# Random-feature attention and two MLPs on one core: projections by head in half the array's rows, products in half its columns, squares of the first batch as products

## The chip, the cores and the metric

The kernel runs on one core of one Trainium2 chip. The time is the device time of one launch in microseconds, the median of several runs; lower is better. One further run is profiled.

## What is computed

Attention with positive random features (4 batches, 8 heads, 576 tokens, head size 64, 128 features) is followed by two MLPs without biases, 512 to 2048 to 512, on the 2304 tokens.

```python
q_s, k_s = (q * scale, k * scale)            # scale = 64 ** -0.25
def phi(x):
    proj = np.einsum('bhsd,md->bhsm', x, omega)
    sq = np.sum(x * x, axis=-1, keepdims=True) / 2.0
    h = proj - sq
    h = h - np.max(h, axis=-1, keepdims=True)
    return np.exp(h) / np.sqrt(m)
q_p, k_p = (phi(q_s), phi(k_s))
kv = np.einsum('bhsm,bhsd->bhmd', k_p, v)
z = np.sum(k_p, axis=2)
num = np.einsum('bhsm,bhmd->bhsd', q_p, kv)
den = np.einsum('bhsm,bhm->bhs', q_p, z)[..., None] + 1e-06
x = num / den                                # tokens x 512
x = softplus(x @ w_in) @ w_out               # first MLP
x = silu(x @ w_in2) @ w_out2                 # second MLP
```

## The kernel before, in words

**Blocks.** The first MLP goes over five token blocks: block b (0 to 3) has the 512 first tokens of batch b, block 4 the 4 x 64 tokens that are left. A block has 16 steps: `gemm1` makes 128 rows of the hidden layer (12 matmuls, three for each of four chunks, since a number is split into a high and a low float32r part), ScalarE applies the softplus twice (once rounded), VectorE takes the difference as the low part, and `gemm2` adds the step's part to four banks of PSUM (12 matmuls). The second MLP does the same with the SiLU on what the first one stored in DRAM.

**Attention.** What block b needs of the attention is computed while block b - 1 runs; that of block 0 before any MLP step, in what is called the opening here. It comes in halves: one half is 256 tokens by four heads of k or of q (`k_half`, `q_half`), or 128 tail tokens of two batches by eight heads (`k_tail`). For each half `inputs` loads x with the head dimension on the partitions (`xT`: two heads below each other, 64 rows each) and once more with tokens on the partitions (`xN`); ScalarE squares `xN` and VectorE sums the squares of each head (`sums`). `features` then works in two groups e:

- `project` (TensorE): features of two heads at once, `xT` as the 128 x 128 stationary operand and the block-diagonal 128 x 256 matrix `om_sb` as the moving one. [...] 
- `top` and `shift` (VectorE): the maximum of each token and head, and the bias from the maximum and the sum of squares in two small operations (L417, L418).
- the exponential (ScalarE): with the bias for each of four heads in batches 0 and 1 (L429), else after a VectorE addition, both groups in one instruction (L439, L446).

A half of k is multiplied with v and a column of ones (`kv`, L489; 65 columns move) and added to the sums `kvs` of its batch. A half of q is transposed (`flip`, L541, tiles `pq`), copied by ScalarE to `qt`, multiplied with `kvs` (`num`, L553, tiles `pn`), divided by its last column on VectorE (`norm`), transposed back (`back`, L575, tiles `px`) and split into the block's x. The tail of q does `num` in column halves (L557: 64 of 128 stationary columns each, for two batches).

**Order.** A class `Order` decides the order of the instructions of PE, ACT, DVE and SP ahead of time. Each item has an engine, a cost, what it depends on, tiles of rings (`BUFS`) and a due time that is propagated backwards; the item that can start first is taken, among equals that with the earliest due time. Weights are loaded as int64 words of float64 numbers and converted on ScalarE and VectorE (L284 to L301 and `diff`, L209), those of the first MLP mostly during block 0.

Of the kernel before, what the change touches and what calls it, by code (L numbers as in the profile page):

```python
# [18 lines left out]
P = 128  # L19
# [17 lines left out]
BUFS = {"wt": 16, "xt": 2, "ghl": 3, "b4": 4, "g": 2, "f": 2, "ld": 3, "b2": 4, "sq": 9, "mn": 6, "den": 3, "bank": 4, "y": 4}  # L37
# [3 lines left out]
G1, G2, G3 = 0.2267, 0.117, 0.224  # L41
# [4 lines left out]
PIPE = 0.25  # L46
RATE = 380e3
ARRIVE = 2.0
ISSUE = 0.5
BEGIN = 45.0  # L50


class Order:
# [5 lines left out]
    def add(self, eng, cost, fn, deps=(), due=None, alloc=(), uses=(), table=None, nbytes=0, after=0.0, loose=False, behind=None):  # L59
        occ, lag = cost if isinstance(cost, tuple) else (cost, PIPE)  # L60
        i = len(self.items)
        it = dict(
            i=i, eng=eng, occ=occ, lag=lag, fn=fn, deps=[d for d in deps if d is not None], due=due,
            alloc=list(alloc), table=table, nbytes=nbytes, after=after, loose=loose, behind=behind, start=None, end=None,
        )
# [9 lines left out]
    def propagate(self):  # L75
# [115 lines left out]
def attention_moe_moe_kernel(  # L191
# [18 lines left out]

    E = mybir.EngineType
# [8 lines left out]
    home = {"wt": pool, "xt": pool, "b4": pool, "ghl": pool, "g": odd, "f": odd, "ld": odd, "b2": odd, "sq": odd, "mn": odd, "den": odd, "bank": psum, "y": psum}  # L220
# [27 lines left out]
    for layer in range(2):  # L248
        for sb in range(NSB):
            full = width[sb] == 2 * T  # L250
            for fc in range(NFC):
                due1[layer, sb, fc] = t
                t += (24 * G1 if full else 12 * (G2 + (G1 / 2 if layer else G2))) + ((1.9 if sb else 2.2) if layer == 0 and sb < B else 0)
    due1["end"] = t

    def bits_pair():
        nc.scalar.copy(bd[:, 0], om_sb)
        diff(bd[:, 1], om_sb, bd[:, 0].bitcast(F32))
# [62 lines left out]
    def inputs(s, name, xT, xN, vs, simple, held, after):  # L321
# [25 lines left out]
        ln = add("SP", (ISSUE, 0), load_n, rv, alloc=[] if here else [tn], uses=[tn] if here else [], nbytes=P * 2048, after=after)  # L347
# [12 lines left out]
        def square():  # L360
            nc.scalar.activation(s["nat"], s["nat"], AF.Square)
# [4 lines left out]

        tsq = new("sq")
        sq = add("ACT", A5, square, [ln], uses=[tn])
        red = add("DVE", V5, sums, [sq], alloc=[tsq], uses=[tn])
        if simple:  # L370
            return lx, tx, red, tsq, lv, tv
        th = new("b4")

        def high():
            s["hl"] = get("b4", [P, 2, 512], F32R, f"hl_{name}")
            nc.scalar.copy(s["hl"][:, 0, :], s["xt"])

        def low():
            diff(s["hl"][:, 1, :], s["xt"], s["hl"][:, 0, :].bitcast(F32))

        h = add("ACT", A5, high, [lx], alloc=[th], uses=[tx])
        l = add("DVE", V5, low, [h], alloc=[], uses=[tx, th])
        return l, th, red, tsq, lv, tv

    def features(s, name, simple, ins, cols, sq_of, psums):
# [5 lines left out]
        for e in range(2):  # L391
            tp, tm = new(psums()), new("mn")

            def project(e=e, tp=tp):
                pp = s["pp", e] = get(tp["tag"], [P, 4, M], F32, f"pp_{name}_{e}")
                for i in range(2):
                    o = pp[:, 2 * i : 2 * i + 2, :].rearrange("p j m -> p (j m)")
                    cs = slice(cols[e][i], cols[e][i] + P)
                    if simple:
# [7 lines left out]
            def top(e=e):  # L407
                s["mn", e] = get("mn", [P, 8], F32, f"mn_{name}_{e}")
                nc.vector.tensor_reduce(s["mn", e][:, :4], s["pp", e], op=ALU.max, axis=AX.X)  # L409

            def shift(e=e):
                s["nb", e] = s["mn", e][:, 4:]
                m3 = s["mn", e][:, :4].rearrange("p (c j) -> p c j", c=2)
                n3 = s["nb", e][:, :4].rearrange("p (c j) -> p c j", c=2)
                sq = sq_of(s["sq"], e)
# [4 lines left out]
            p = add("PE", 4 * G3 if simple else 6 * G2, project, [x, const_ready], alloc=[tp], uses=[tx])  # L420
            m = add("DVE", V5, top, [p], alloc=[tm], uses=[tp])
            n = add("DVE", VS, shift, [m, red], uses=[tm, tsq])
            if simple:
                tphi = new("b2")

                def exp(e=e):
                    phi = get("b2", [P, 4, M], F32, f"phi_{name}_{e}")
                    for i in range(4):
                        nc.scalar.activation(phi[:, i], s["pp", e][:, i], AF.Exp, bias=s["nb", e][:, i : i + 1])  # L429
                    s["phi", e] = phi  # L430
# [4 lines left out]
            def shifted(e=e):  # L435
                if e == 0:
                    s["both"] = get("b4", [P, 2, 4, M], F32, f"phi_{name}")
                nb = s["nb", e][:, :4].unsqueeze(2).to_broadcast([P, 4, M])
                nc.vector.tensor_tensor(s["both"][:, e], s["pp", e], nb, op=ALU.add)  # L439

            adds.append(add("DVE", V5, shifted, [n] + adds, alloc=[tboth] if e == 0 else [], uses=[tp, tm] + ([tboth] if e else [])))
# [29 lines left out]
    def k_half(n, half, simple, psums, due, after):  # L471
# [3 lines left out]
        ins = inputs(s, name, kT[n, :, 2 * half : 2 * half + 2, :], kN[n, :, :, hs, :], [(v1[n, :, :, hs, :], (2, 4))], simple, simple, after)  # L475
        cols, sq_of = main_cols()
        phis = features(s, name, simple, ins, cols, sq_of, psums)
        tk = new(psums())
        b, h0 = n // 2, 4 * half
        both = []  # L480
        for e, (x, tphi) in enumerate(phis):

            def kv(e=e):
                phi, v = s["phi", e], s["v", 0]
                if "pkv" not in s:
                    s["pkv"] = get(tk["tag"], [P, 4, D + 1], F32, f"pkv_{name}")
                for j in range(2):
# [5 lines left out]
            both.append(add("PE", 4 * G3, kv, [x, ins[4][0]] + both, alloc=[] if e else [tk], uses=[tphi, ins[5][0]] + ([tk] if e else [])))  # L493
        chain(b, h0, add("DVE", VH, lambda: kv_add(b, h0, s["pkv"]), both, due=due, uses=[tk]))

    def k_tail(bp, simple, psums, due, after):
# [3 lines left out]
        ins = inputs(s, name, kT[NT, :, :, bp * P : (bp + 1) * P], kN[NT, :, bp], vs, simple, simple, after)  # L500
        cols = [(2 * u * P, 2 * u * P + P) for u in range(2)]
        phis = features(s, name, simple, ins, cols, lambda sq, u: sq[:, 4 * u : 4 * u + 4].rearrange("p (c j) -> p c j", c=2), psums)
        for u, (x, tphi) in enumerate(phis):
            for i in range(2):
                tk = new(psums())

                def kv(u=u, i=i, tk=tk):
                    phi, v = s["phi", u], s["v", u]
                    pkv = s["pkv", u, i] = get(tk["tag"], [P, 2, 2, D + 1], F32, f"pkv_{name}_{u}_{i}")
                    for j in range(2):  # L510
                        nc.tensor.matmul(
                            pkv[:, j].rearrange("p a d -> p (a d)"), phi[:, 2 * i + j, :],
# [3 lines left out]
                k = add("PE", 2 * G3, kv, [x, ins[4][u]], alloc=[tk], uses=[tphi, ins[5][u]])  # L516
# [5 lines left out]
    def q_half(n, half, simple, psums, due, after):  # L522
# [327 lines left out]
```

## Time and profile before

| | us |
|---|---|
| median of 3 runs | 972.95 (972.69 to 976.61) |
| profiled execution | 972.0 |
| its span, first to last instruction | 970.2 |
| TensorE busy | 943.5 (97%) |
| ScalarE busy | 443.3 (46%) |
| VectorE busy | 427.6 (44%) |
| mean granted TensorE clock | 0.994 of full speed |

Busy time counts the union of an engine's instructions. Matmuls overlap in their pipeline, so the duration of one is longer than its share of the stream; the distance between the starts of two is that share.

### The profile page before, as it was taken

What the parts mean: (1) busy time and instruction counts of PE and PEld (TensorE: products, weight loads), DVE (VectorE), ACT (ScalarE), POOL (GpSimd) and SP (SyncE); (2) the same over time, 40 slices, a digit from 0 to 9 for tenths busy, and PEclk for the clock granted to TensorE, in tenths of its full rate; (3) what the DMA queues carried; (4) which work ended last, traced back from release to release, by engine and by line L of the source; (5) the groups of instructions that cost most, each with busy time, mean ns of one, the idle gap of its engine ahead of it and who ended that gap; (6) DMA issues with size and microseconds to landing.
All of it is one profiled execution on the core that took longest, in us unless ns stands there. A gap on an engine that the chain in (4) does not pass through costs nothing.

```text
span 970.2 us, 12523 instructions
## 1 busy us (share of the span) xinstructions
PE 943.5 (97%) x4936; PEld 803.3 (83%) x4936; DVE 427.6 (44%) x923; ACT 443.3 (46%) x810; POOL 1.2 (0%) x7
## 2 busy tenths in 40 slices
PE   8899999999999999999999999999999999999994
PEld 7678778888888888887889988888888888888893
DVE  6987889455535453442112999521111112111210
ACT  7888878555555555442213776332222122221220
POOL 0000000000000000000000000000000000000000
PEclk9999999999999999999999999999999999999998
DMA  9643443222012221010003666202002000100100
GB/s 332 217 141 131 154 151 109 87 88 77 22 34 77 78 65 33 1 45 1 0 1 131 217 197 217 75 12 76 0 9 79 1 1 11 60 1 6 44 1 22
DMA packets 38159, 72.86 MB, mean 75 GB/s; under 512 B 3412, under 2 KB 18388, under 8 KB 38100
## 3 DMA queue, kind: packets, MB, share of 16 engines
q1 hardware_dynamic: 37970, 71.79, 22.0%
q8 instruction: 39, 0.64, 0.3%
q10 hardware_dynamic: 130, 0.26, 0.1%
q14 instruction: 20, 0.16, 0.1%
HBM read 62.60 MB, written 9.44 MB: 74 GB/s over the span
## 4 chain that ended last, share of the span: by engine, by line
PE 86%; DVE 5%; ACT 5%; DMA 2%; issue 1%; SPq 0%; ACTq 0%; DVEq 0%
PE y L664 20%; PE y L656 18%; PE h L633 13%; PE h L635 13%; PE h L634 13%; PE pkv_k L489 2%; PE pn_q L553 2%; PE pq_q L541 1%; DMA xN_q<-in_qN 1%; ACT phi_k L429 1%; DVE wt L209 1%; DVE wf L292 1%; ACT L641 1%; ACT L429 1%; PE px_q L575 1%
## 5 line engine op out<-in xcount | busy, mean ns | idle before, releaser
L209 DVE TENSOR_TENSOR ghl<-g,ghl 128x512 fp32r<-128x512 f32 (+1 forms) x160 | 101.9, 637 | 413.1 <-ACT ghl L642 411.6
L641 ACT ACTIVATE g<-h 128x512 f32<-128x512 f32 (+1 forms) x160 | 88.6, 554 | 333.4 <-PE h L635 332.9
L633 PE MATMUL h<-x,wt 128*128 128x512 f32 (+1 forms) x640 | 238.2, 372 | 0.4 <-ACT ghl L642 0.4
L634 PE MATMUL h<-x,wt 128*128 128x512 f32 (+1 forms) x640 | 235.8, 368 | 0.9 <-DVE x L209 0.9
L635 PE MATMUL h<-x,wt 128*128 128x512 f32 (+1 forms) x640 | 236.0, 369 | 0.0
L656 PE MATMUL y<-ghl,wt 128*128 128x512 f32 (+1 forms) x960 | 213.8, 372 | 0.0
L664 PE MATMUL y<-wt,ghl 128*128 128x512 f32 x864 | 208.6, 390 | 0.0
L656 PEld LDWEIGHTS y<-ghl,wt 128*128 128x128 f32 x960 | 166.2, 189 | 28.4
L664 PEld LDWEIGHTS y<-wt,ghl 128*128 128x128 f32 x864 | 161.3, 188 | 32.8
L634 PEld LDWEIGHTS h<-x,wt 128*128 128x128 f32 x640 | 120.8, 189 | 21.0 <-DVE x L209 1.3
L633 PEld LDWEIGHTS h<-x,wt 128*128 128x128 f32 x640 | 120.7, 189 | 20.4 <-ACT ghl L642 0.8
L635 PEld LDWEIGHTS h<-x,wt 128*128 128x128 f32 x640 | 120.7, 189 | 20.4
L642 ACT ACTIVATE ghl<-h 128x512 fp32r<-128x512 f32 (+1 forms) x160 | 88.1, 550 | 35.7 <-PE y L664 29.3
L284 ACT ACTIVATE wf<-raw 128x512 f32<-128x512 f32 x64 | 43.1, 681 | 13.8 <-DVE wt L209 13.5
L301 ACT CAST wt<-wf 128x512 fp32r<-128x512 f32 x64 | 39.4, 624 | 16.4 <-DVE wf L296 15.9
L209 DVE TENSOR_TENSOR wt<-wf,wt 128x512 fp32r<-128x512 f32 x64 | 43.2, 685 | 5.3 <-ACT wt L301 5.2
L292 DVE SCALAR_TENSOR_TENSOR wf<-wf,raw 128x512 uint32<-128x512 uint32 x64 | 43.0, 685 | 1.5 <-ACT wf L284 1.1
L296 DVE SCALAR_TENSOR_TENSOR wf<-raw,wf 128x512 uint32<-128x512 uint32 x64 | 43.1, 684 | 0.2
L641 ACT ACT_TABLE_LOAD x29 | 37.2, 1283 | 11.8 <-PE h L635 11.5
L409 DVE TENSOR_REDUCE mn_q<-pp_q 128x4 f32<-128x512 f32 x36 | 24.4, 686 | 24.3 <-PE pp_q L405 24.3
L553 PEld LDWEIGHTS pn_q<-kv,qt_q 128*128 128x128 f32 x256 | 30.8, 192 | 5.0 <-ACT qt_q L545 4.1
L553 PE MATMUL pn_q<-kv,qt_q 128*128 128x65 f32 x256 | 31.2, 275 | 2.4 <-ACT qt_q L545 2.4
(103 smaller groups left out, 708.8 us busy)
## 6 DMA issues: line engine op xcount, KB each, us to landing
raw<-in_w SPq DMA_DIRECT2D x64, 512.0 KB, 3.7
out<-y_sb SPq DMA_DIRECT2D x17, 256.0 KB, 2.2
y_dram<-y_sb SPq DMA_DIRECT2D x16, 256.0 KB, 2.0
x2raw<-y_dram SPq DMA_DIRECT2D x16, 256.0 KB, 3.8
xT_q<-in_qT SPq DMA_DIRECT2D x14, 256.0 KB, 2.9
xN_q<-in_qN SPq DMA_DIRECT2D x14, 256.0 KB, 3.1
x_k<-in_v SPq DMA_DIRECT2D x8, 260.0 KB, 5.3
v_k<-in_v SPq DMA_DIRECT2D x8, 260.0 KB, 3.0
```

The costliest lines, as they stand in the source:

```text
L209: nc.vector.tensor_tensor(o, a, b, op=ALU.subtract)
L284: nc.scalar.activation(s["f"], hif, AF.Copy, scale=2.0**-112)
L292: nc.vector.scalar_tensor_tensor(fu, fu, 3, lo, op0=ALU.logical_shift_left, op1=ALU.bitwise_or)
L296: nc.vector.scalar_tensor_tensor(fu, hi, 0x80000000, fu, op0=ALU.bitwise_and, op1=ALU.bitwise_or)
L553: nc.tensor.matmul(pn[:, i, :], qt[:, i, :], kvs[n // 2][:, h, :], start=True, stop=True)
L633: nc.tensor.matmul(ph[:, :w], wt[:, 0, 0, cs], xt[:, 0, cc, :w], start=(cc == 0), stop=False)
L634: nc.tensor.matmul(ph[:, :w], wt[:, 0, 0, cs], xt[:, 1, cc, :w], start=False, stop=False)
L635: nc.tensor.matmul(ph[:, :w], wt[:, 0, 1, cs], xt[:, 0, cc, :w], start=False, stop=(cc == NCC - 1))
L641: nc.scalar.activation(g, s["h"][:, :w], f)
L642: nc.scalar.activation(ghl[:, 0, :w], s["h"][:, :w], f)
L656: nc.tensor.matmul(py[dm][:, :w], wt[:, 1, a, cs], g[:, x, :w], start=(first and i == 0), stop=(last and i == 2),)
L664: nc.tensor.matmul(py[c], g[:, x, cs], wt[:, 1, a, :], start=(first and i == 0), stop=(last and i == 2),)
```

## The change

Eight edits:

1. `project` multiplies each head by itself: the 64 rows of `xT` that hold head j of a pair, with the same 64 rows of a 128-column omega (`om_sb` holds it twice, one below the other). The two heads of a pair follow each other, write different banks of PSUM and stand in different rows of the array. It is float32 in all batches; the split of x and omega (`hl`, `bd`) is gone. A half's groups are now its heads by parity j, four heads each.
2. In the first batch (`fold`: k and q of n < 2, and the first k tail) ScalarE squares `xT`, and a second product of the squares with a matrix of -scale^2/2 (`neg_half`) is added to the projection, so that the maximum alone, negated, is the bias. The load of `xN`, `sums` and `shift` are gone there.
3. `kv` of the main tokens and `num` of the main tokens are done in column halves by `by_halves`.
4. `project` is one item for both groups; it writes two banks. The flips wait for both groups' exponentials.
5. The features of batches 0 and 1 have a ring `ph` of their own (4); `ghl` has 2 buffers for 3, `b4` 3 for 4.
6. Projections of batch 0 use the ring `y` alone, everything else `bank`.
7. Planning: costs `G4`, extra lead `wait` (`AHEAD`, `WAIT`), `BEGIN` 36 for 45, 1.4 for 1.9 a step in blocks 1 to 3.
8. The second MLP's weights may be loaded from the start (`after` 0.0).

```diff
-BUFS = {"wt": 16, "xt": 2, "ghl": 3, "b4": 4, "g": 2, "f": 2, "ld": 3, "b2": 4, "sq": 9, "mn": 6, "den": 3, "bank": 4, "y": 4}
+BUFS = {"wt": 16, "xt": 2, "ghl": 2, "b4": 3, "g": 2, "f": 2, "ld": 3, "b2": 4, "ph": 4, "sq": 9, "mn": 6, "den": 3, "bank": 4, "y": 4}
...
+    def by_halves(o, a, b, **flags):
+
+        for c in range(2):
+            r = slice(c * 64, c * 64 + 64)
+            nc.tensor.matmul(o[r], a[:, r], b, **flags)
...
-    bd = const.tile([P, 2, 2 * M], F32R, name="bd")
-    om_sb = const.tile([P, 2 * M], F32, name="om_sb")
-    nc.sync.dma_start(om_sb, om)
+    om_sb = const.tile([P, M], F32, name="om_sb")
+    for j in range(2):
+        nc.sync.dma_start(om_sb[j * D : (j + 1) * D, :], om[j * D : (j + 1) * D, j * M : (j + 1) * M])
...
-        ln = add("SP", (ISSUE, 0), load_n, rv, alloc=[] if here else [tn], uses=[tn] if here else [], nbytes=P * 2048, after=after)
+        ln = None if fold else add("SP", (ISSUE, 0), load_n, rv, alloc=[] if here else [tn], uses=[tn] if here else [], nbytes=P * 2048, after=after)
...
-            nc.scalar.activation(s["nat"], s["nat"], AF.Square)
+            nc.scalar.activation(s["nat"], s["xt"] if fold else s["nat"], AF.Square)
...
-                    if simple:
-                        nc.tensor.matmul(o, s["xt"][:, cs], om_sb, start=True, stop=True)
-                    else:
-                        hl = s["hl"]
-                        nc.tensor.matmul(o, hl[:, 0, cs], bd[:, 0, :], start=True, stop=False)
-                        nc.tensor.matmul(o, hl[:, 0, cs], bd[:, 1, :], start=False, stop=False)
-                        nc.tensor.matmul(o, hl[:, 1, cs], bd[:, 0, :], start=False, stop=True)
...
+            for q, c in enumerate(cols):
+                for j in range(2):
+                    r = slice(j * D, (j + 1) * D)
+                    nc.tensor.matmul(pp[j][:, q], s["xt"][r, c : c + P], om_sb[r, :], start=True, stop=not fold)
+                if fold:
+                    for j in range(2):
+                        r = slice(j * D, (j + 1) * D)
+                        nc.tensor.matmul(pp[j][:, q], s["nat"][r, c : c + P], neg_half[r, :], start=False, stop=True)
...
+                if fold:
+                    s["nb", j] = s["mn", j]
+                    nc.vector.tensor_reduce(s["mn", j][:, :4], s["pp"][j], op=ALU.max, axis=AX.X, negate=True)
...
-                        nc.tensor.matmul(
-                            s["pkv"][:, 2 * e + j], phi[:, 2 * c + j, :], v[:, c, 2 * e + j, :], start=(c == 0), stop=(c == 1)
-                        )
+                        by_halves(s["pkv"][:, 2 * e + j], phi[:, 2 * e + c, :], v[:, c, 2 * e + j, :], start=(c == 0), stop=(c == 1))
...
-                        nc.tensor.matmul(pn[:, i, :], qt[:, i, :], kvs[n // 2][:, h, :], start=True, stop=True)
+                        by_halves(pn[:, i, :], qt[:, i, :], kvs[n // 2][:, h, :], start=True, stop=True)
...
-                    weights(1, fc, io, due1[0, NSB - 1, 0] + 2.8 * fc + 2.0)
+                    weights(1, fc, io, 0.0)
```

What this does to the order is seen in three places. The first is the start of VectorE's list; `mn` are the maxima, `sqs` the sums of squares, `pp` the projections. Before:

```order
L409 TENSOR_REDUCE mn_k_0_0_123<-pp_k_0_0_114 128x4
L365 TENSOR_REDUCE sqs_k_0_126<-x_k_0_94 128x8
L409 TENSOR_REDUCE mn_k_0_1_133<-pp_k_0_1_120 128x4
L417 SCALAR_TENSOR_TENSOR mn_k_0_0_123<-sqs_k_0_126,mn_k_0_0_123 128x4
L418 SCALAR_TENSOR_TENSOR mn_k_0_0_123<-sqs_k_0_126,mn_k_0_0_123 128x4
L417 SCALAR_TENSOR_TENSOR mn_k_0_1_133<-sqs_k_0_126,mn_k_0_1_133 128x4
L418 SCALAR_TENSOR_TENSOR mn_k_0_1_133<-sqs_k_0_126,mn_k_0_1_133 128x4
```

And now, the first two halves:

```order
L414 TENSOR_REDUCE mn_k_0_0_159<-pp_k_0_0_117 128x4
L414 TENSOR_REDUCE mn_k_0_1_165<-pp_k_0_1_118 128x4
L414 TENSOR_REDUCE mn_k_0_0_179<-pp_k_0_0_140 128x4
L414 TENSOR_REDUCE mn_k_0_1_192<-pp_k_0_1_141 128x4
L469 COPY kv_90<-pkv_k_0_181 128x260
```

Of seven operations for a half of the first batch two are left.

The second is on TensorE in block 0, around its ninth step; `y` is gemm2 (four rows are one), `pn` the product of q features with the sums, `px` the transposition back. Before:

```order
L656 MATMUL y_0_3_797<-ghl_0_7_1240,wt_7_1059 128x512 x3
L553 MATMUL pn_q_1_0_1357<-kv_89,qt_q_1_0_1333 128x65 x4
L553 MATMUL pn_q_1_1_1364<-kv_89,qt_q_1_1_1348 128x65 x4
L633 MATMUL h_0_9_1377<-x_0_487,wt_9_1229 128x512
L634 MATMUL h_0_9_1377<-x_0_487,wt_9_1229 128x512
L635 MATMUL h_0_9_1377<-x_0_487,wt_9_1229 128x512
```

Nine more rows of that gemm1 (`h_0_9`) stand ahead of the `px` that reads what VectorE made of `pn`. Now:

```order
L659 MATMUL y_0_3_915<-ghl_0_7_1386,wt_7_1313 128x512 x3
L217 MATMUL pn_q_1_0_1503<-kv_91,qt_q_1_0_1474 64x65 x8
L217 MATMUL pn_q_1_1_1521<-kv_91,qt_q_1_1_1489 64x65 x8
L578 MATMUL px_q_1_1532<-ident,xn_q_1_0_1517 128x128 x2
L397 MATMUL pp_q_0_0_1536<-om_sb,xT_q_0_1199 128x128
L397 MATMUL pp_q_0_1_1537<-om_sb,xT_q_0_1199 128x128
L397 MATMUL pp_q_0_0_1536<-om_sb,xT_q_0_1199 128x128
L397 MATMUL pp_q_0_1_1537<-om_sb,xT_q_0_1199 128x128
```

The `px` follows the second `pn` at once, and the gemm1 of that step comes after the next gemm2.

The third is on TensorE one step later: the flips `pq` of the last half of q in block 0, whose projection `pp_q_1` is the first row. Now:

```order
L397 MATMUL pp_q_1_1_1696<-om_sb,xT_q_1_1419 128x128
L578 MATMUL px_q_0_1690<-ident,xn_q_0_1_1688 128x128 x2
L659 MATMUL y_0_0_912<-ghl_0_9_1623,wt_9_1519 128x512 x3
L659 MATMUL y_0_1_913<-ghl_0_9_1623,wt_9_1519 128x512 x3
L659 MATMUL y_0_2_914<-ghl_0_9_1623,wt_9_1519 128x512 x3
L659 MATMUL y_0_3_915<-ghl_0_9_1623,wt_9_1519 128x512 x3
L544 MATMUL pq_q_1_0_1757<-ident,phi_q_1_0_1737 128x128
```

Before, a whole gemm1 (twelve rows) stood between that gemm2 and the flips; now it comes after them.

## Rows read from the trace of the kernel before

**Rows 1.** Busy time by stage (columns in the first row): opening, blocks 0 to 4.

```profile
core 0: us, PE busy (x) PEld busy (x) DVE busy (x) ACT busy (x) POOL busy (x), PEclk, DMA share, GB/s
0.00:53.94 53.94, 47.10 (x276) 38.77 (x277) 44.11 (x127) 40.31 (x109) 1.16 (x7) 0.97 0.76 262
53.94:177.23 123.29, 119.85 (x619) 100.77 (x618) 100.08 (x222) 99.91 (x189) 0.00 (x0) 1.00 0.38 128
177.23:301.65 124.42, 124.42 (x697) 108.15 (x696) 61.75 (x149) 66.70 (x92) 0.00 (x0) 1.00 0.19 60
301.65:417.54 115.89, 115.89 (x645) 100.36 (x644) 56.85 (x132) 62.74 (x87) 0.00 (x0) 1.00 0.17 53
417.54:513.79 96.25, 93.98 (x485) 77.75 (x484) 19.75 (x40) 27.30 (x45) 0.00 (x0) 1.00 0.03 11
513.79:559.72 45.93, 45.93 (x373) 45.44 (x372) 30.27 (x60) 25.51 (x57) 0.00 (x0) 1.00 0.53 184
```

**Rows 2.** The same columns for the opening from its sixth microsecond on.

```profile
20.00:34.00 14.00, 13.20 (x89) 11.50 (x87) 13.35 (x47) 12.29 (x37) 0.00 (x0) 1.00 0.97 348
34.00:53.94 19.94, 16.60 (x102) 13.76 (x103) 18.63 (x51) 14.72 (x36) 0.00 (x0) 0.91 0.45 147
sum 47.94, PE 42.87 PEld 36.67 DVE 43.69 ACT 37.80 POOL 0.00; mean PE 14.29 PEld 12.22 DVE 14.56 ACT 12.60 POOL 0.00
```

**Rows 3.** Timeline of TensorE in the opening: start, duration, instructions merged.

```profile
15.88 1.08 PE L400 MATMUL pp_k<-om_sb,x_k 128*128 128x256 f32 x4
16.80 1.00 PE L489 MATMUL pkv_k<-x_k,phi_k 128*128 128x65 f32 x8
17.64 1.08 PE L400 MATMUL pp_k<-om_sb,x_k 128*128 128x256 f32 x4
```

**Rows 4.** Timeline in block 1: split projections.

```profile
203.83 0.29 PE L405 MATMUL pp_k<-bd,hl_k 128*128 128x256 f32 x1
...
204.19 0.28 PE L405 MATMUL pp_k<-bd,hl_k 128*128 128x256 f32 x1
```

**Rows 5.** Chain that ended last, in order of time: start, duration.

```profile
484.03 2.72 PE y L656 x12
```

**Rows 6.** Timeline in block 3 around the column halves (PEld: weight loads).

```profile
447.54 0.39 PE L635 MATMUL h<-x,wt 128*128 128x512 f32 x1
447.85 1.01 PEld L557 LDWEIGHTS pn_q<-kv,qt_q 128*64 128x64 f32 x32 [0.35 <-issue]
...
449.14 0.69 DVE L209 TENSOR_TENSOR ghl<-g,ghl 128x512 fp32r<-128x512 f32 x1 [4.25 <-ACT ghl L642]
...
450.72 0.30 PE L575 MATMUL px_q<-ident,xn_q 128*128 128x128 f32 x1 [1.71 <-DVE den_q L564]
```

**Rows 7.** Durations of line L557: ns min/median/max.

```profile
L557 PEld LDWEIGHTS pn_q<-kv,qt_q x64: 132/138/142, 424.0 to 448.7; 128*64 128x64 f32 x64
```

**Rows 8.** Timeline of VectorE in the opening.

```profile
7.19 0.68 DVE L365 TENSOR_REDUCE sqs_k<-x_k 128x8 f32<-128x512 f32 x1
7.78 0.68 DVE L409 TENSOR_REDUCE mn_k<-pp_k 128x4 f32<-128x512 f32 x1
8.38 0.15 DVE L417 SCALAR_TENSOR_TENSOR mn_k<-sqs_k,mn_k 128x4 f32<-128x4 f32 x1
...
8.95 0.69 DVE L409 TENSOR_REDUCE mn_k<-pp_k 128x4 f32<-128x512 f32 x1
```

**Rows 9.** The page's costliest groups: table loads of ScalarE.

```profile
L641 ACT ACT_TABLE_LOAD x29 | 37.2, 1283 | 11.8 <-PE h L635 11.5
```

**Rows 10.** Timeline of ScalarE in the opening, idle time before in brackets.

```profile
5.59 0.63 ACT L361 ACTIVATE x_k<-x_k 128x512 f32<-128x512 f32 x1 [1.91 <-DMA x_k<-in_kN]
8.44 0.63 ACT L361 ACTIVATE x_k<-x_k 128x512 f32<-128x512 f32 x1 [2.22 <-DMA x_k<-in_kN]
...
15.84 1.12 ACT L429 ACTIVATE phi_k<-pp_k,mn_k 128x128 f32<-128x128 f32 x4
```

**Rows 11.** Longest of TensorE's waits in block 0: total, times, longest one.

```profile
PE pn_q L553 <- ACT qt_q L545: 2.2, 2, 1.3
```

More of the change, by code (lines that the diff above doesn't have):

```diff
@@ L46 @@
 PIPE = 0.25
+AHEAD, WAIT = 3, 2
 RATE = 380e3
@@ L57, in __init__, with add @@
         self.items = []
-    def add(self, eng, cost, fn, deps=(), due=None, alloc=(), uses=(), table=None, nbytes=0, after=0.0, loose=False, behind=None):
+    def add(self, eng, cost, fn, deps=(), due=None, alloc=(), uses=(), table=None, nbytes=0, after=0.0, loose=False, behind=None, wait=0.0):
         occ, lag = cost if isinstance(cost, tuple) else (cost, PIPE)
@@ L63, in add @@
             i=i, eng=eng, occ=occ, lag=lag, fn=fn, deps=[d for d in deps if d is not None], due=due,
-            alloc=list(alloc), table=table, nbytes=nbytes, after=after, loose=loose, behind=behind, start=None, end=None,
+            alloc=list(alloc), table=table, nbytes=nbytes, after=after, loose=loose, behind=behind, wait=wait, start=None, end=None,
         )
@@ L87, in propagate @@
                 due = min(due, n["due"] - n["occ"] - it["lag"])
+            due -= it["wait"]
             if it["nbytes"]:
@@ L319, in attention_moe_moe_kernel, with inputs @@
     kv_last = {}
-    def inputs(s, name, xT, xN, vs, simple, held, after):
+    def inputs(s, name, xT, xN, vs, fold, held, after):
         here = new("wt") if held else None
@@ L360, in square @@
         def square():
-            nc.scalar.activation(s["nat"], s["nat"], AF.Square)
+            if fold and not here:
+                s["nat"] = get("ld", [P, 512], F32, f"xq_{name}")
+            nc.scalar.activation(s["nat"], s["xt"] if fold else s["nat"], AF.Square)
         def sums():
@@ L365, in sums @@
             nc.vector.tensor_reduce(s["sq"], s["nat"].rearrange("p (c d) -> p c d", d=D), op=ALU.add, axis=AX.X)
+        if fold:
+            sq = add("ACT", A5, square, [lx], alloc=[] if here else [tn], uses=[tx] + ([tn] if here else []))
+            return lx, tx, sq, tn, lv, tv
         tsq = new("sq")
@@ L369, in inputs, with features @@
         red = add("DVE", V5, sums, [sq], alloc=[tsq], uses=[tn])
-        if simple:
[L371 to L385, printed above, removed]
+        return lx, tx, red, tsq, lv, tv
+    def features(s, name, simple, fold, ins, cols, sq_of, psums):
         x, tx, red, tsq, _, _ = ins
@@ new lines, in features, with project @@
+        tps = [new(psums) for _ in range(2)]
+        def project():
+            pp = [get(tp["tag"], [P, 4, M], F32, f"pp_{name}_{j}") for j, tp in enumerate(tps)]
+            s["pp"] = pp
+            for q, c in enumerate(cols):
[6 more added lines that the diff above has]
+                        nc.tensor.matmul(pp[j][:, q], s["nat"][r, c : c + P], neg_half[r, :], start=False, stop=True)
@@ new lines, in features, with top, shift @@
+        if fold:
+            p = add("PE", 16 * G4, project, [x, red], alloc=tps, uses=[tx, tsq], wait=AHEAD)
+        else:
+            p = add("PE", 8 * G4, project, [x], alloc=tps, uses=[tx], wait=WAIT)
+        for j in range(2):
+            tp, tm = tps[j], new("mn")
+            def top(j=j):
+                s["mn", j] = get("mn", [P, 8], F32, f"mn_{name}_{j}")
+                if fold:
+                    s["nb", j] = s["mn", j]
+                    nc.vector.tensor_reduce(s["mn", j][:, :4], s["pp"][j], op=ALU.max, axis=AX.X, negate=True)
+                else:
+                    nc.vector.tensor_reduce(s["mn", j][:, :4], s["pp"][j], op=ALU.max, axis=AX.X)
+            def shift(j=j):
+                s["nb", j] = s["mn", j][:, 4:]
+                sq = sq_of(s["sq"], j)
+                m3 = s["mn", j][:, :4].rearrange("p (a b) -> p a b", a=2)
+                n3 = s["nb", j][:, :4].rearrange("p (a b) -> p a b", a=2)
@@ L423, in features, with exp @@
             if simple:
[L424 to L430, printed above, removed]
+                tphi = new("ph")
+                def exp(j=j):
+                    phi = get("ph", [P, 4, M], F32, f"phi_{name}_{j}")
+                    for q in range(4):
+                        nc.scalar.activation(phi[:, q], s["pp"][j][:, q], AF.Exp, bias=s["nb", j][:, q : q + 1])
+                    s["phi", j] = phi
@@ L532, in q_half @@
             xready[0, sb] = []
-        tx = new(psums())
+        tx = new("bank")
         backs = []
-        for e, (x, tphi) in enumerate(phis):
-            tq, tn, tqs, td, txn = new(psums()), new(psums()), new("b2"), new("den"), new("b2")
+        for e in range(2):
+            tq, tn, tqs, td, txn = new("bank"), new("bank"), new("b2"), new("den"), new("b2")
             def flip(e=e, tq=tq):
```

98 lines of the change are left out of this document (36 added, 62 removed).

## The prediction

> **What bounds the kernel now.** I first cut the span at the starts of the five blocks of the first MLP [rows 1]. In blocks 0 to 2 TensorE is busy 119.9 of 123.3, 124.4 of 124.4 and 115.9 of 115.9 us; in block 4 it is 45.9 of 45.9, and from there on the matmuls and their order are as they were. So in blocks 0 to 2 a microsecond of TensorE work is a microsecond of time, as long as no new wait opens. The opening (0 to 53.94) is another case: in its later part VectorE is busy 13.35 of 14 and 18.63 of 19.94 us, TensorE 13.2 and 16.6, ScalarE 12.29 and 14.72 [rows 2]. VectorE is the tightest there, ScalarE not far behind. In block 0 VectorE and ScalarE are at 100 of 123 us as well, since they convert the weights; in blocks 1 and 2 they have half their time free [rows 1].
>
> The matmul durations of the page are latencies; the price of one is the distance between starts. Two projection matmuls of the float32 kind (four instructions: each float32 matmul is two) take from 15.88 to 16.80, 0.92; four head products (eight instructions) from 16.80 to 17.64, 0.84, so 0.105 for each load of 128 columns with 65 columns moving [rows 3]. Three matmuls of the split kind take 203.83 to 204.19, 0.12 each [rows 4]. Twelve of a GEMM take 2.72 [rows 5].
>
> **What each part costs.** Before, a half (four heads of 256 tokens) projects for 2 x 0.92 = 1.84 us, or, split, 12 x 0.12 = 1.44.
>
> *Column halves.* The tail of q already does its products in column halves (L557): 32 loads of 64 columns lie in 1.01 us with 0.138 for one [rows 6, 7], so (1.01 - 0.138)/31 = 0.028 each. Two halves run side by side, else a head would cost what it does whole. A group of four heads is now 16 loads: 0.45 instead of 0.84.
>
> *Row halves.* No row of before has two matmuls in different rows of the array. Two heads' instructions, if they overlap as the column halves do, take one 128-column load, 0.105; if not, 0.21. A half is 8 such pairs: 0.84, or 1.68 at worst; with the squares as products 1.68, or 3.36. I take the overlap, by the nearest rows [rows 6, 7], and keep the other end.
>
> *Switches.* These halves stand between whole-array work, and that is not free. Ahead of L557 the last whole matmul starts at 447.54; a next one would follow 0.23 later, but the load starts 0.31 later with 0.35 of "issue" idle in front [rows 6]: 0.09 late, and the first 64-column load (about 0.05) has nothing to hide behind. That is 0.14 for a switch. The Trainium skill, TensorEngine Tiling (Array Packing), section Key Properties, says that changing the tiling mode drains the engine; the trace agrees with those 0.14 us, and it is the rule that speaks against this change: without it, on the speed of concurrent tiles alone, the sum below would be 16 us lower (rival 2). The order of after has 24 changes of kind (whole, rows, columns) on TensorE in the opening, then 33, 36, 33 and 6 in blocks 0 to 3 (before: 4, in block 3). I price all at 0.14, bounds 0 and 0.28, since the way back and rows are not in the trace.
>
> Work on TensorE, counted in both orders:
> - Opening: before 10 halves x 1.84 and 16 groups x 0.84 = 31.8; after 9 x 1.68 + 0.84 + 18 x 0.45 = 24.1; -7.7, switches +3.4.
> - Block 0: 7 x 1.84 + 1.44 + 16 x 0.84 = 27.7; after 8 x 0.84 + 14 x 0.45 = 13.0; -14.7, switches +4.6.
> - Block 1: 9 x 1.44 + 13.4 = 26.4; after 9 x 0.84 + 7.2 = 14.8; one gemm2 of 2.72 fewer in it; -14.3, switches +5.0.
> - Block 2: 8 x 1.44 + 13.4 = 24.9; after 13.9; one gemm2 more, two flips more (0.9); -7.4, switches +4.6.
> - Block 3: one half 1.44 to 0.84, two flips fewer; -1.5, switches +0.3.
>
> *New waits.* Products are shorter and stand closer to what needs them. Where px follows pn with no GEMM between, TensorE waits for the three VectorE steps: 1.71 us before, where a 0.69 subtraction stood ahead of them [rows 6]; 1.3 at about 0.4 less. The order of after does this twice in block 0 and once in block 1, with a GEMM there before: +2.6 and +1.3. In block 0 one pair of flips comes one gemm2 (2.72) and little else after its projection, where before a gemm1 lay between too. The chain is two maxima of 0.60, four shifts 0.57 [rows 8], a table load 1.28 [rows 9] and two exponential groups (1.1 and about 1.0) [rows 10], 5.2 in all: 2.2 us late. In block 3 the px that waited 1.71 now has a gemm between: -1.7.
>
> *Opening.* VectorE loses for each of 9 halves a reduction (0.60) and four shifts (0.57) [rows 8]: 10.5 us. TensorE loses 7.7 - 3.4 = 4.3. ScalarE loses nothing: nine squares stay, two exponential groups of the next batch come forward (+2). Its two waits for the natural-order load, 1.91 and 2.22 [rows 10], shrink with that load gone. From 5.6 us on it has 37.8 us of work [rows 2], back to back a little less, plus 2: not before 45 us. So of 10.5 us VectorE can give at most 9, TensorE alone 4; I take 5, and block 0 starts at 49.
>
> *At nothing:* in blocks 1 and 2 the split's cast and subtraction go, on engines with half their time free. The feature ring of two lets the softplus of step n+2 start only when gemm2 of step n is done; that gemm2 stands ahead of gemm1 of n+2 or one GEMM behind it, and its piece is needed 5.4 us later, for 2 us of work: covered. Raw weights have three buffers for four; block 0 converts 32 in 120 us. The second MLP's weights may be loaded earlier, but their tiles are held by the first MLP's until block 4. If such cover failed, a step would lose up to 2 us.
>
> **Sum.** Opening -5; block 0 -14.7 + 4.6 + 4.8 = -5.3; block 1 -14.3 + 5.0 + 1.3 = -8.0; block 2 -2.8; block 3 -1.5 + 0.3 - 1.7 = -2.9: -24.0 from a span of 970.2, 946.2. The profiled execution took 972.0, 1.8 over its span, so 948; the median of the runs is 0.95 above that: **949 us**.
>
> **Rivals.**
> 1. *Row halves don't overlap.* For it: no row shows it. Against: column halves do. Then 26 halves of blocks 0 to 3 cost 0.84 more, 21.8 us, and the opening gets 16 us more on TensorE, of which its slack hides some 5: 949 + 22 + 11 = 982, slower. It decides from a pair of about 0.18 us on (208 pairs in the blocks, about 100 of the opening's uncovered, against 24 us). The Trainium skill, TensorE: Matmul & The Clock Gate, Part 3, has row groups run concurrently, four at 3.07 times; by 3.07/4 of the ideal for a pair a half would be 1.1 us, and the time some 10 us more than 949, an estimate; no row here shows it.
> 2. *Switches cost nothing* where they are not the measured kind, or hide in waits: 16 us less, 933.
> 3. *Vector and scalar work hold the opening and block 0.* Block 0 still has 100 us of VectorE work in order, and weights in both queues; if it stays at 123.3 and the opening at 54, 10.3 come back: 959. For it: 81% busy in 123 us would be 85% in 118. Against: the longest group of TensorE's waits in block 0 is 2.2 us now [rows 11].
> 4. *Switches at 0.28 and rival 3 together*: 959 + 14 = 973, no change.
>
> The granted clock was 0.91 at the end of the opening [rows 2]; with thinner work there it may fall for longer. TensorE would then need up to twice the time in the last third (some 8 us of work in 17): hidden, or 2 us.
>
> **Chances.** Forecast 0.60 (own range 938 to 956), rival 2 0.12, rival 3 0.12, rival 4 0.06, rival 1 0.10. A difference under 0.5% (5 us) can't be told from no change here. Faster 0.84, same 0.06, slower 0.10. The range 930 to 966 leaves out rivals 1 and 4 and little at the low end.
>
> **What would show it.** Row pairs: starts of the two heads' projection instructions within 0.02, pairs 0.105 to 0.12 apart; 0.21 is rival 1. Column groups of 16 in about 0.45. "Issue" idle of 0.3 to 0.4 before loads at changes of kind, on the way back too. First gemm1 at 46 to 51; block 0 near 118, block 1 near 116, block 2 near 113, block 3 near 93, the rest unchanged. VectorE below ScalarE in the opening. Wrong if a half's projection takes over 1.4 us, if block 0 stays near 123, or if the second MLP changes.

## The result, and the profile after

The changed kernel takes 959.14 us (median of 4 runs, 957.68 to 959.78), the kernel before beside it 972.82: ratio of the means 0.9853, 95% interval 0.982 to 0.9885. It takes 14 us or 1.5% less, with the interval clear of 1, and not the 24 us less that were forecast. 959 is inside the stated range (930 to 966) and outside the forecast's own (938 to 956).

The profiled execution took 959.57 us, its span 957.8 (before 970.2); TensorE is busy 926.5 us of it, ScalarE 431.9, VectorE 406.7, at a mean clock of 0.989. Busy time by stage, cut as in [rows 1]:

```profile
core 0: us, PE busy (x) PEld busy (x) DVE busy (x) ACT busy (x) POOL busy (x), PEclk, DMA share, GB/s
0.00:53.77 53.77, 45.24 (x660) 38.59 (x660) 37.48 (x90) 41.50 (x117) 1.31 (x8) 0.95 0.63 214
53.77:173.38 119.61, 113.95 (x776) 90.28 (x775) 96.38 (x210) 92.43 (x176) 0.00 (x0) 0.98 0.42 135
173.38:293.03 119.65, 117.19 (x850) 95.01 (x849) 55.72 (x139) 62.10 (x83) 0.00 (x0) 1.00 0.20 63
293.03:407.41 114.38, 114.38 (x824) 92.69 (x823) 51.19 (x123) 60.29 (x82) 0.00 (x0) 1.00 0.17 54
407.41:500.49 93.08, 93.08 (x484) 76.49 (x483) 23.29 (x49) 26.63 (x45) 0.00 (x0) 1.00 0.13 40
500.49:547.12 46.63, 46.19 (x373) 45.46 (x372) 34.03 (x65) 26.72 (x60) 0.00 (x0) 1.00 0.48 162
547.12:957.80 410.68, 396.51 (x1851) 332.14 (x1849) 108.59 (x184) 122.26 (x229) 0.00 (x0) 0.99 0.13 44
```

| | before | forecast | after |
|---|---|---|---|
| opening | 53.94 | -5 | 53.77 (-0.2) |
| block 0 | 123.29 | -5.3 | 119.61 (-3.7) |
| block 1 | 124.42 | -8.0 | 119.65 (-4.8) |
| block 2 | 115.89 | -2.8 | 114.38 (-1.5) |
| block 3 | 96.25 | -2.9 | 93.08 (-3.2) |
| block 4 | 45.93 | 0 | 46.63 (+0.7) |

Blocks 0 to 2 gave 55 to 70% of what was forecast, block 3 all of it; the opening gave nothing (its first gemm1 matmul starts at 53.92 us; before, at 53.95). Its later rows, to set beside [rows 2]:

```profile
6.00:20.00 14.00, 14.00 (x252) 13.13 (x252) 6.54 (x12) 12.40 (x40) 0.00 (x0) 1.00 1.04 372
20.00:34.00 14.00, 13.98 (x231) 12.82 (x227) 12.41 (x32) 11.76 (x35) 0.00 (x0) 1.00 0.59 199
34.00:53.77 19.77, 13.19 (x184) 11.10 (x182) 18.53 (x48) 15.12 (x41) 0.00 (x0) 0.87 0.43 134
```

VectorE's saved time lies in the first row: 6.54 busy of 14 us, where it was 11.71 (the sum in [rows 2] less its two other stretches). There TensorE is busy without a gap. From 34 us on VectorE is as full as before.

TensorE in block 2: a column group (kv), a row half (projection), then gemm2 again.

```profile
309.73 0.61 PE L659 MATMUL y<-ghl,wt 128*128 128x512 f32 x2
310.27 0.69 PE L217 MATMUL pkv_k<-v_k,phi_k 128*64 128x65 f32 x16
310.89 1.16 PE L397 MATMUL pp_k<-om_sb,xT_k 64*128 64x128 f32 x16
311.98 1.21 PE L659 MATMUL y<-ghl,wt 128*128 128x512 f32 x4
```

The group takes 0.62 to the next start and the half 1.09, each with one change of kind. By the records of the whole trace a group goes from first to last start in 0.46 and a half in 0.89; behind whole work both start 0.09 late, behind a group of columns the next starts 0.12 late, behind one of rows 0.15. Over the 132 changes that is 0.12 on average.

Single instructions (two for a float32 product) show the sign that the prediction had named: the two heads' instructions start 0.007 apart and the next two 0.112 after them; only the second two of a half follow at 0.21.

The opening's end and the first step of block 0, by clock:

```profile
48.00:52.22 4.22, 1.96 (x20) 1.19 (x20) 4.01 (x15) 1.61 (x5) 0.00 (x0) 1.00 0.76 247
52.22:59.05 6.83, 6.31 (x28) 4.86 (x28) 6.69 (x13) 5.80 (x12) 0.00 (x0) 0.50 0.50 155
```

TensorE is busy 1.96 of 4.22 us, then its granted clock is 0.50 (1.2 of 2.4 GHz) for 6.83 us, which hold the first gemm1. Its matmuls stand 0.43 apart instead of 0.23.

TensorE's longest waits in block 0 and, below, VectorE's (total, times, longest):

```profile
PE px_q L578 <- DVE den_q L567: 2.8, 1, 2.8
PE h L638 <- DVE wt L211: 1.1, 2, 0.6
...
DVE raw L294 <- DMA raw<-in_w: 11.9, 7, 3.5
DVE ghl L211 <- ACT ghl L645: 4.1, 3, 3.6
```

VectorE waits 11.9 us for raw weights to land. Before, with four buffers for them, it was 0.9 in the whole of block 0:

```profile
DVE raw L288 <- DMA raw<-in_w: 0.9, 2, 0.6
```

The timeline shows how one such wait becomes TensorE's:

```profile
127.77 0.69 DVE L211 TENSOR_TENSOR wt<-wf,wt 128x512 fp32r<-128x512 f32 x1
129.91 0.43 DVE L294 TENSOR_SCALAR raw<-raw 128x512 uint32<-128x512 uint32 x1 [1.46 <-DMA raw<-in_w]
130.26 0.68 DVE L211 TENSOR_TENSOR ghl<-g,ghl 128x512 fp32r<-128x512 f32 x1
133.39 0.43 DVE L294 TENSOR_SCALAR raw<-raw 128x512 uint32<-128x512 uint32 x1 [2.45 <-DMA raw<-in_w]
133.73 0.68 DVE L373 TENSOR_REDUCE sqs_q<-xN_q 128x8 f32<-128x512 f32 x1
134.33 0.15 DVE L567 TENSOR_SCALAR den_q<-pn_q 128x4 f32<-128x4 f32 x1
...
131.37 1.15 PE L217 MATMUL pn_q<-kv,qt_q 128*64 128x65 f32 x32
...
135.30 0.41 PE L578 MATMUL px_q<-ident,xn_q 128*128 128x128 f32 x2 [2.78 <-DVE den_q L567]
```

The `pn` that `den` reads was issued from 131.37 on, but `norm` is queued behind the weight that lands at 133.39.

### The profile page after: what moved, and what is told of

It is laid out like the page before. It is cut to its first block, busy times and chain, and to the rows that moved or that the text cites. A ratio compares the mean times of both kernels' runs of the same rounds, so it can differ in the third digit from the quotient of the medians.

```text
span 957.8 us, 14259 instructions
## 1 busy us (share of the span) xinstructions
PE 926.5 (97%) x5804; PEld 770.7 (80%) x5804; DVE 406.7 (42%) x858; ACT 431.9 (45%) x788; POOL 1.3 (0%) x8
## 4 chain that ended last, share of the span: by engine, by line
PE 84%; DVE 7%; DMA 4%; ACT 2%; SPq 1%; issue 1%; DVEq 0%; ACTq 0%
PE y L667 20%; PE y L659 18%; PE h L636 13%; PE h L638 13%; PE h L637 13%; DMA raw<-in_w 3%; PE pkv_k L217 1%; PE pp_q L397 1%; PE pp_k L397 1%; PE pq_q L544 1%; PE pn_q L217 1%; DVE wf L302 1%; DVE wt L211 1%; DVE wf L298 1%; PE px_q L578 1%
## 5 line engine op out<-in xcount | busy, mean ns | idle before, releaser
L290 ACT ACTIVATE wf<-raw 128x512 f32<-128x512 f32 x64 | 43.6, 686 | 23.1 <-DVE wt L211 13.7
L294 DVE TENSOR_SCALAR raw<-raw 128x512 uint32<-128x512 uint32 x64 | 26.8, 423 | 20.5 <-DMA raw<-in_w 20.3
L416 DVE TENSOR_REDUCE mn_q<-pp_q 128x4 f32<-128x512 f32 x28 | 18.7, 685 | 25.1 <-PE pp_q L397 25.1
```

Of the source, the lines that this page charges most:

```text
L290: nc.scalar.activation(s["f"], hif, AF.Copy, scale=2.0**-112)
```

## The experiments

All start from the changed kernel. Opening and block 0 also stand together, since most of what one gained the other gave back. Stages are read from one profiled execution of each kernel. The last two columns say how long the granted clock was 0.50 in it: in opening and block 0, and in block 1.

| run | time, us (range) | opening | block 0 | together | block 1 | block 2 | half clock, opening and block 0 | half clock, block 1 |
|---|---|---|---|---|---|---|---|---|
| changed kernel | 959.14 (957.68 to 959.78) | 53.77 | 119.61 | 173.38 | 119.65 | 114.38 | 10.2 | 0 |
| e1_one_head_first | 982.92 (982.33 to 983.51) | 62.75 | 124.46 | 187.21 | 125.48 | 118.68 | 13.7 | 3.4 |
| e2_num_whole | 965.95 (965.16 to 967.04) | 54.45 | 120.14 | 174.59 | 122.37 | 116.61 | 10.2 | 3.4 |
| e3_kv_whole | 967.16 (966.35 to 968.48) | 56.59 | 121.36 | 177.95 | 123.05 | 116.03 | 13.7 | 3.4 |
| e4_no_fold | 961.06 (959.23 to 962.24) | 50.27 | 123.31 | 173.58 | 121.13 | 114.38 | 10.2 | 3.4 |
| e5_hold_next | 958.28 (957.95 to 958.32) | 48.82 | 123.15 | 171.97 | 119.67 | 114.38 | 6.8 | 0 |
| e8_fill | 957.78 (956.84 to 959.39) | 54.67 | 117.83 | 172.50 | 121.10 | 114.38 | 6.8 | 3.4 |
| e9_late_w1 | 961.88 (960.45 to 963.05) | 52.68 | 121.82 | 174.50 | 121.24 | 114.38 | 10.2 | 3.4 |
| e11_b4_4_b2_3 | 957.65 (957.23 to 959.93) | 52.88 | 118.10 | 170.98 | 120.95 | 114.37 | 6.8 | 3.4 |
| e12_no_fold_b4_4 | 959.54 (958.91 to 959.86) | 51.90 | 120.97 | 172.87 | 121.00 | 114.37 | 13.7 | 3.4 |
| e12_hold_next_b4_4 | 957.99 (955.73 to 959.58) | 50.64 | 122.14 | 172.78 | 120.69 | 114.37 | 6.8 | 3.4 |
| e13_no_sign | 954.73 (954.12 to 955.30) | 52.73 | 115.53 | 168.26 | 120.85 | 114.37 | 3.4 | 3.4 |
| e14_fill_b4_4 | 956.19 (954.86 to 956.96) | 52.62 | 116.07 | 168.69 | 120.33 | 114.37 | 0 | 3.4 |

Block 2 has no such stretch in the changed kernel and repeats within 0.01 us in the nine experiments that leave its products alone. In block 1 one stretch of 3.4 us makes the difference: e8's 121.10 is 1.45 longer than the changed kernel's, e5, without one, has 119.67. So differences of 1 to 2 us between stages can be the clock's, and the times of e4, e5, e8, e11 and both e12 overlap those of the changed kernel.

**Rows: one head first.**

```diff
-            for q, c in enumerate(cols):
-                for j in range(2):
-                    r = slice(j * D, (j + 1) * D)
+            for j in range(2):
+                r = slice(j * D, (j + 1) * D)
+                for q, c in enumerate(cols):
```

> The four projections of the even head stand ahead of the four of the odd head, so neighbours on TensorE lie in the same rows of the array; same work, same results. Theory A (two heads' products run side by side because neighbours lie in different rows): a half takes 1.79 instead of 0.90 from its first start to its last, the 26 halves of blocks 0 to 3 cost 23 us more, the opening hides a part of its own; in all 980 to 990. Rival B (a matmul on 64 rows is simply twice as fast, or instructions that write different banks overlap): a half keeps 0.90, the time stays within 2 us of 959.

Theory A. The same place in block 2:

```profile
331.09 1.71 PE L397 MATMUL pp_k<-om_sb,xT_k 64*128 64x128 f32 x16
332.73 0.96 PE L657 MATMUL y<-ghl,wt 128*128 128x512 f32 x3
```

The half takes 1.64 to the next start instead of 1.09, and block 2 with its eight halves is 4.3 longer, 0.54 each. Instructions in the same rows stand 0.112 apart, as far as the pairs in alternate rows: two heads side by side cost what one head costs. First to last start is still 1.44, not 1.79: in the middle of each half three instructions start 0.004 to 0.006 behind another, as those of two heads do in the changed kernel, so some overlap where the heads meet. So the blocks lost less than expected (block 0 4.9, block 1 5.8, block 2 4.3), and the opening, where TensorE sets the pace early, 9.0. Each head writes a bank of its own, so this run changed the order of banks with that of rows, and the banks of rival B are not tried by themselves. On the whole array banks alone don't do it: gemm2 goes from bank to bank with its matmuls 0.23 apart throughout.

**Columns: num whole, then kv whole.**

```diff
-                        by_halves(pn[:, i, :], qt[:, i, :], kvs[n // 2][:, h, :], start=True, stop=True)
+                        nc.tensor.matmul(pn[:, i, :], qt[:, i, :], kvs[n // 2][:, h, :], start=True, stop=True)
```

> The product of q features with the sums is one whole matmul again, kv stays in halves; same results. Theory A (a change of kind costs 0.13 on TensorE, as the changed kernel's starts read): a group of four heads takes 0.84 instead of 0.46 and saves two changes, some 0.12 net a group in the blocks, where groups stand in pairs or behind flips 0.3; in all 2 to 6 us more than 959. Rival B (changes hide in work that is there anyway): 0.38 for each of 30 groups, the time 9 or more above 959.

The second makes the same replacement at `kv` in `k_half`.

> kv of the main tokens as whole matmuls, num stays in halves; same results. Theory A (0.13 for a change of kind): a group of two heads' pairs takes 0.84 instead of 0.46 plus 0.26 for two changes, 0.12 more for each of 24 groups in blocks 0 to 2, 3 us in all; the time 960 to 963. Rival B (changes cost nothing): 0.38 each, 9 us; the time 966 or more.

The first came out at 6.8 us over, just above A's 6; the second at 8.0, B's size. Block 2, where TensorE has no waits in the changed kernel, decides: 2.23 and 1.65 longer. For kv, eight groups of 0.83 instead of 0.49 are 2.7 more; the missing 1.1 is the price of 10 changes of kind (33 in the changed kernel's block 2, 23 here): 0.11 each. Changes cost, as in A; the expectation's fault was to count two for each group. Many groups lie next to a row half, and there only about one change is saved. The 2.8 us that the second run lost in the opening are in neither theory, which had left out the opening's ten kv groups: TensorE is busy 48.1 us there instead of 45.2. Some of both times is clock, as the table's last columns show.

**The fold undone.**

```diff
-        exps, tphis = features(s, name, simple, sb == 0, ins, cols, sq_of, psums)
+        exps, tphis = features(s, name, simple, False, ins, cols, sq_of, psums)
```

(so in `q_half`, `k_half` and `k_tail`, and for `fold` in their calls of `inputs`)

> The squares of batch 0 are summed on VectorE again (natural-order load, sums, two shifts), and no product of squares stands on TensorE; all else as in the changed kernel. Theory A (what VectorE saved fell into the first 20 us, where it waits for TensorE, and bought nothing at the end of the opening): the opening is 52 to 56 us long, the time 957 to 962. Rival B (it did save some 5 us, and another edit lost them again): the opening is 59 or longer, the time 964 or more.

Neither: the time, 961.06, is in A's range, but the opening is 3.5 us shorter without the fold. Its row from 6 to 20 us:

```profile
6.00:20.00 14.00, 11.98 (x194) 10.02 (x192) 11.90 (x34) 11.22 (x38) 0.00 (x0) 1.00 1.05 361
```

VectorE is busy 11.90 of 14 us instead of 6.54, TensorE 11.98 instead of 14. The folded products kept VectorE waiting for its maxima. But block 0 gave the 3.5 back.

**The next batch's first half held.**

```diff
+            hold[:] = xready[0, 0] if b == 1 and f is k_half else []
...
-            p = add("PE", 8 * G4, project, [x], alloc=tps, uses=[tx], wait=WAIT)
+            p = add("PE", 8 * G4, project, [x] + hold, alloc=tps, uses=[tx], wait=WAIT)
```

(the same for its squares)

> The first half of k of the next batch may not begin its squares or projection before batch 0 is done, so its maxima, exponentials and kv move behind the first step of block 0. Theory A (VectorE is the bound at the end of the opening, and this half stands in its way and ahead of the first gemm1): block 0 starts at 49 to 51 instead of 53.77 and gives part of it back, the time 955 to 959. Rival B (the last half of batch 0 sets the start by itself): the start stays within 1 us, the time within 1 us of 959 or above.

Theory A for the start: 48.82, what the prediction had forecast (49), and for the time. Block 0 again gave back 3.5 of the 5.0; the held half itself now lies there, where TensorE is busy 117.3 us instead of 114.0.

**The clock held by products without use.**

```diff
+                if n == 1 and half == 1 and e == 1:
+                    for _ in range(9):
+                        nc.tensor.matmul(bank[:, 384:], ident, ident, start=True, stop=True)
```

(three more behind the first `kv` of batch 1)

> Nine float32 products of the identity with itself (about 2 us, results unused) stand behind the last num of batch 0, where TensorE waits 2.2 us, and three (about 0.7) behind the first kv of the next batch, where it waits 0.6. Theory A (the half clock from 52.2 to 59.05 follows from the empty 48 to 52): the clock stays full there, the first gemm1s run at 0.23 a matmul instead of 0.43, block 0 is 2 to 3 us shorter and the time 956 to 957. Rival B (the clock falls for another reason, or work without use does not hold it): block 0 within 0.7 us of 119.6, the time 959 to 960.

The same two stretches:

```profile
48.00:52.22 4.22, 3.42 (x34) 2.72 (x30) 3.85 (x14) 1.18 (x4) 0.00 (x0) 1.00 0.70 224
52.22:59.05 6.83, 6.83 (x67) 5.40 (x66) 6.76 (x14) 6.30 (x15) 0.00 (x0) 1.00 0.55 170
```

With TensorE busy 3.42 of 4.22 us the clock stays full. Block 0 is 1.8 shorter, not 2 to 3, and the time 0.8 above the range. In this run other stretches of half clock came, 3.4 us each: at 12 us, in an opening that is 0.9 longer, at 135 us, and in block 1 at 251.

**Weights of steps 1 and 2 later** (`0.0 if fc < 1 else` for `0.0 if fc < 3 else`).

> Weights of steps 1 and 2 are loaded by their due times instead of from the start, so four conversions of six may leave the opening. Theory A (opening and block 0 share one stream of conversions): the opening is 1 to 4 us shorter and block 0 as much longer, together 172 to 174.5, the time 958 to 960. Rival B (the attention's own chain sets the end of the opening): the opening stays within 0.7 of 53.77, and nothing is gained or lost elsewhere.

Stages as in theory A: opening 1.1 shorter, block 0 2.2 longer; the time is 2 us above the range given.

**Four raw buffers** (`"b4": 4`, `"b2": 3`).

> Four buffers for raw weights again instead of three; the room comes from a buffer less of the ring b2 (three for four: copies of flips, normed heads, results on their way out). Theory A (in block 0 VectorE stands before raw weights that land late, 11.5 us in all, with the normalization that TensorE needs behind it): VectorE's wait for raw weights falls under 3 us, TensorE's longest px wait of 2.8 and half of its 1.1 for weights go, block 0 is 116 to 117 and the time 955 to 957. Rival B (VectorE's and ScalarE's work itself paces block 0): the waits only change their name and block 0 stays at 119 to 120.

Half of A: VectorE's wait for raw weights falls from 11.9 to 7.5, not under 3, TensorE's longest px wait from 2.8 to 1.3, together 2.4 shorter. Its 1.1 for weights became 1.6. Block 0 and the time stay 1.1 and 0.7 above A's ranges, and before the change that first wait was 0.9. Four buffers under the two edits that had shortened the opening:

> No squares as products, and four buffers for raw weights with three of b2. Without the fold alone the opening fell to 50.27 and block 0 rose to 123.31, 173.58 together. Theory A (the raw weights' ring is what gave those 3.5 us back): opening 49.5 to 51 and block 0 at most 120, 170.5 or less together, the time 955 to 957. Rival B (the conversions' own work sets when block 0 can end): together 173 or more, the time 959 or more.

> The next batch's first half held until batch 0 is done, and four buffers for raw weights with three of b2. Held alone the opening was 48.82 and block 0 123.15, 171.97 together. Theory A: opening 48.5 to 49.5, block 0 at most 120, 169 or less together, the time 953 to 955. Rival B (conversions pace block 0): together 171.5 or more, the time 957 or more.

Theory B in both, 172.78 and 172.87 together (the run without the fold is 0.13 short of B's 173). In both TensorE waits for the low part of a weight until 150 us, in the changed kernel, e4 and e5 until 149 to 151, whenever block 0 began.

**Less conversion work.**

```diff
+            if layer == 0:
+                return
             _, hi, fu = views()
             nc.vector.scalar_tensor_tensor(fu, hi, 0x80000000, fu, op0=ALU.bitwise_and, op1=ALU.bitwise_or)
```

> The last of VectorE's steps on a weight of the first MLP (putting the sign back, 0.60 us) is left out, so the first MLP computes with weights without sign; the order of all other instructions is the same. VectorE has 32 x 0.60 = 19 us less to do until block 0 ends, and a raw buffer is free 0.6 earlier. Theory A (conversions and the raw weights' ring pace the opening from 23 us on and block 0): opening and block 0 together 169.5 or less instead of 173.38, the time 955 or less. Rival B (TensorE's own stream, clock and the order set the pace): together 172 or more, the time 958 or more.

Theory A, by 5.1 us together:

```profile
20.00:52.73 32.73, 26.15 (x418) 23.04 (x416) 28.22 (x73) 27.03 (x76) 0.00 (x0) 0.99 0.54 187
52.73:168.26 115.53, 112.38 (x776) 89.59 (x775) 81.01 (x183) 91.98 (x176) 0.00 (x0) 0.99 0.40 135
```

In block 0 VectorE is busy 81.01 us instead of 96.38, its wait for raw weights falls to 2.9, and TensorE's for the low parts from 1.1 to 0.2. Half of the 5.1 goes with the clock: at half speed TensorE ran here for 3.4 us in the two stages, not 10.2, and it is busy 2.6 us less with the same matmuls. The other 2.5 are waits: in block 0 it idles 3.15 us instead of 5.66.

**Fill and four buffers together** (both edits as above).

> The twelve products without use that kept the clock up, and four buffers for raw weights with three of b2. If the two losses are separate, they add up: opening 53 to 54.7, block 0 at most 116.5, together 170 or less, the time 955 to 956.5. If both only move the point at which block 0 waits for its weights (147 to 150 us in all runs so far), together stays at 171 or more and the time at 957 to 958.

They add up, and more: 168.69, 4.7 less, where e8 alone gave 0.9 and e11 2.4. The opening's 52.62 is 0.4 below its range. No stretch of half clock lies in the two stages, where e8 and e11 had 6.8 us each; the first comes in block 1:

```profile
240.74:244.15 3.41, 2.97 (x8) 2.33 (x9) 3.01 (x7) 2.22 (x3) 0.00 (x0) 0.50 0.01 2
```

At 956.19 it is the fastest of the kernels that leave nothing out, and its runs lie below those of the changed kernel, which were measured at another time. The ratios to the kernel before, measured beside each, are 0.9831 (0.9799 to 0.9862) and 0.9853 (0.982 to 0.9885): these overlap. Its longest waits in block 0, TensorE's and then VectorE's:

```profile
PE px_q L586 <- DVE den_q L575: 1.4, 1, 1.4
PE h L646 <- DVE wt L211: 1.2, 2, 0.7
...
DVE raw L294 <- DMA raw<-in_w: 5.6, 4, 2.0
```

## Why the prediction was right, and where it was 10 us off

**What was right.** Row halves overlap, and columns do (rivals 1 and 2 fall). A change of kind was priced at 0.14 and is 0.12 by the starts, 0.11 by taking kv's halves away. The Trainium skill, TensorEngine Tiling (Array Packing), Key Properties, has the engine drained when the mode changes. Both numbers agree in that each change costs; no run shows the drain itself. TensorE's time did set blocks 2 and 3. That the time lies in the stated range is owed to its width: the 0.60 forecast, 938 to 956, missed it.

**The step that failed is the opening's -5.** It took half of VectorE's 10.5 us for time on the path. VectorE's busy time in the opening fell by 6.6 us only, 5.2 of it between 6 and 20 us, where the folded projections made TensorE the pace (e4: without the fold VectorE fills that stretch and the opening is 3.5 shorter). At the end the next batch's first half, which the change brought forward, stood ahead of the first gemm1 (e5: 5.0, of which block 0 gave back 3.5). The sum counted TensorE's work over the opening, not where in it.

**The second is "at nothing" for three raw buffers.** The cover named, 32 weights in 120 us, is an average. VectorE runs in a fixed order, so a weight that lands late holds up the `norm` behind it; a fourth buffer (e11) is worth 2.4 us in the two stages, part of it perhaps clock, and leaves 7.5 us of that wait where there was 0.9 before. Behind it is rival 3's mechanism: the stream of conversions holds opening and block 0 together. e4, e5 and both e12 shorten the opening and lose most of it, or more, in block 0; e13, with 19 us less for VectorE, wins 5.1, half of it with the clock. Rival 3's 959 is the time that came, though not by its terms: block 0 did shrink by 3.7.

**The third is the clock**, "hidden, or 2 us". It was not hidden: the first gemm1, 12 matmuls 0.43 apart instead of 0.23, takes 5.3 us instead of 2.7, 2.6 more; e8 and e14 keep the clock full there.

**Terms of a wrong size.** A half takes 0.95 with its own last distance, not 0.84 (its pairs stand 0.112 apart, not 0.105, and the second starts 0.10 late), a group 0.49, not 0.45, a change 0.12, not 0.14. In block 2 (8 halves, 16 groups, 33 changes) that is 0.9 + 0.7 - 0.7 of a shortfall of 1.3. In block 1 (9, 16, 36) it is 1.0 + 0.7 - 0.7, and TensorE waits 2.3 us for px, not 1.3: 2.0 of 3.2. In block 0 (8, 14, 33) it is 0.9 + 0.6 - 0.7, with 2.6 of clock and 1.3 of waits for weights; px and flips cost 4.3, 4.8 were priced, near by luck (the flips 0.6 instead of 2.2, px 3.7 instead of 2.6, with 2.8 of it behind a late weight); and TensorE's waits of before, 2.2 [rows 11], 0.9 and 0.4, are gone, which the sum had not credited. Net that is 0.7 of a shortfall of 1.6. So 0.4, 1.2 and 0.9 us are left unexplained in blocks 2, 1 and 0.

**Open.** Which of the conversions' resources binds near 150 us, the ring, the transfers or VectorE's order, is not settled: e11 and e13 change more than one of them. The order (edits 4, 6 and 7) and the rings of edit 5 other than the raw weights' were not undone by themselves. From block 4's start to the end of the last matmul the changed kernel's trace takes 443.0 us, every experiment's 442.3, as before the change. All of them load the second MLP's weights early and have two `ghl` buffers, so neither costs block 4's 0.7 by itself.

## What to carry to other kernels

Work taken off the busiest engine counts only in the stretch where it is late, so cut the stage finer and ask who waits for whom in each piece. A ring that is shared by a stream of loads is judged by its worst landing and by what is queued behind it, not by its average. Two neighbouring stages that share one stream of work should be summed before a gain in either is believed.

## What the runs showed of the hardware

- Instructions of float32 products on 64 rows with 128 columns moving (two for each product) stand 0.112 us apart in the same rows (e1), and in alternate rows two start 0.007 apart and the next two 0.112 after them (changed kernel). On the whole array such instructions stand 0.112 apart too (the products without use in e8). So half the rows alone save nothing; alternation gives twice the rate, less the 0.10 by which a half's second pair is late.
- By the estimate from the Trainium skill, TensorE: Matmul & The Clock Gate, Part 3, that stood beside rival 1, a half would take 1.1 us; the runs give 0.95.
- A stretch in which TensorE was busy 1.96 of 4.22 us was followed by 6.83 us at half clock, one with 3.42 of 4.22, filled by products without use, was not. No rule is read from this: in e8 half clock came at 135 us after a wait of 2.3 us, in the changed kernel none after one of 2.8.
